# A second pair of PSUM banks for some landmark products, products with v grouped by tile shape, and another order of steps

## The chip, the cores and the metric

The kernel runs on one core of one Trainium2 chip. Its time is the device time of one execution in microseconds (us), as the median of three runs. Beside these runs there is one profiled execution, whose trace gives every instruction of the five engines (TensorE or PE with its weight loads PEld, VectorE or DVE, ScalarE or ACT, GpSimd or POOL, SyncE or SP) and the clock that was granted to TensorE.

## The reference

Three stages are computed in a row, all in float32: a Nystrom attention of 8 batches with 8 heads, 576 tokens and 64 features, then a gated layer, then a layer with an ELU.

```python
# q, k, v: (8, 8, 576, 64); 32 landmarks = means over 18 tokens
q_lm = q.reshape(B, H, 32, 18, D).mean(axis=3)
k_lm = k.reshape(B, H, 32, 18, D).mean(axis=3)
A, Bm, C = sm(q, k_lm), sm(q_lm, k_lm), sm(q_lm, k)     # softmax of scaled products
Z = Bm.T / (norm1(Bm) * norminf(Bm) + 1e-6)             # largest sums of columns and of rows, per head
for _ in range(6):
    Z = 2 * Z - Z @ Bm @ Z
x = A @ Z @ C @ v                                       # to (4608, 512)
h = ((x @ w1) * (x @ w2)) @ w3                          # 512 -> 1024 -> 1024
x = h @ w_out                                           # 1024 -> 512
h = x @ w_in                                            # 512 -> 2048
out = np.where(h > 0, h, np.exp(np.minimum(h, 0)) - 1) @ w_out2   # 2048 -> 512
```

## The kernel before

The kernel has a start, a first layer and a second layer. In the start the weights come from DRAM and are converted (steps `L`, `y`, `r`, `h`, `w`, `x` of one weight tile each: load, two passes on ScalarE, two on VectorE, one on GpSimd), and the product of w3 and w_out is formed once in 16 groups (`o`, L908). Batch 0's attention is worked in between.

The first layer runs over 128 units u, 16 of each batch. A unit is two groups of 12 full-array products of 288 columns: `A` (function `ab`, the two gated products, in the two PSUM banks of the pool `ps_mm`) and `Y` (`yy`, accumulated over 8 units in four banks of `ps_acc`). Between them the gated product is taken off PSUM: `G` (ScalarE copies the first bank), `g` (VectorE multiplies with the second), `D` and `d` (high and low part). The next `A` may write the first bank after `G` and the second after `g`.

Among the units stands the attention of the following batch, written `:b` and a letter. On TensorE these are small products on tiles of part of the array: `c0`, `c1` (landmarks of q with all of k, tile 64x32), `a0`, `a1`, `t0` to `t2` (transposes, full array), `v0`, `v1` (the products with v: 128 and, for the last 64 tokens, 64 rows high, 32 wide), `z`, `m0` to `m3` (the landmark products with the gated layer's weights, tile 64x32, 512 columns, two banks each), and for pairs of batches `b`, `r`, `n0` to `n5` (32 wide). Before the change all of them write the two banks of one pool, `ps_at`: `c1` can write when `C0` (ScalarE) has read `c0`, and `m1` when `M0` (ScalarE, high part) and `l0` (VectorE, low part) have read `m0`. A visit below is one or more small products in a row between full-array groups.

In the second layer the activations are read back from DRAM (`yin`, L1141) and split in parts `YH`/`YL`; rows `R` (L1196 to L1198) are six full-array products each for one of 40 units, rows `OR` (L1290 to L1292) the six products of the output side. Their weights come as `wp` tiles (`WP`, four buffers, queued on SyncE, L1135) and `wh` tiles (queued on GpSimd). `OP` and `OE` add a row's bank to the sums on VectorE, and `OO` stores a result from SyncE's queue.

Every engine works its instructions in the order in which they are written. That order is one list, STEPS: 4418 steps, whose functions are called one after the other. Which of two or three buffers a tile takes is written in a second list, SLOTS; a name that isn't in it takes the buffers in turn. A step that waits holds up all that stands behind it on its engine.

Of the kernel before, what the change touches and what calls it, by code (L numbers as in the profile page):

```python
# [52 lines left out]
h17 o11 r17 r20 o13 :0r :0ce1 h20 r16 L18 :0bx y21 :0R o15 s0 h21 w20 s1 :0ae x16 L19 s2 r21 w17 S0 S1 :0n0 S2
:0N0 w21 s3 x17 S3 :0iv :0au y19 L23 o16 h19 y18 x21 w19 r19 x19 L25 :0af0 :0a1 x20 o17 :0A1 y22 :1iq h22 r22
r25 L27 h18 r23 :0n1 :3S0 y25 o19 w18 h25 w25 r18 :0N1 :0n2 L24 :0am y23 y27 :0as :1k0 :0ae h23 w23 L30 h27
:0N2 L29 y30 :1k2 x25 r27 :0ah0 w27 x18 w22 L26 h30 L33 o21 x23 :0t2 :1q0 y24 :1q3 x27 :0n3 :0T2 x22 y29 r30
L31 h29 r24 o23 :0N3 w30 :0t1 h24 :0T1 y26 w24 x24 :1k3 r26 :0n4 :0N4 y31 h26 w26 :0cn x30 L34 :3L1 y34 h31
o25 r29 L28 x26 :1q2 w31 y33 :0v0 :1k1 L32 :0v1 w29 :0V y28 x29 :0n5 h28 r31 :0N5 w28 x31 r28 o27 h33 w33 :0z
r33 x33 :0Z :0au h34 :3L2 :3S2 o29 w34 :1q1 :0m0 y32 x28 r34 = L35 s4 L39 s7 S7 x34 s6 :0M0 :0l0 r35 :0H0 :0m1
h32 :1p0 :3S1 y35 h35 r32 :0M1 w32 A0 G0 :0l1 y39 g0 x32 h39 :1b A1 G1 s5 r39 :1B w35 w39 D0 L38 x39 g1 S4  # L60
:1c0 :1C0 S5 A2 x35 G2 S6 g2 :1c1 d0 y38 D1 :1C1 D2 d1 r38 h38 A3 :1cm0 :1be G3 L36 :0m2 w38 Y0 Y1 r36 d2 y36
h36 :0M2 L37 g3 x38 D3 :0l2 :2ik A4 :1iv w36 :0af1 G4 g4 :1a0 y37 h37 w37 :1A0 :1am :1cm1 x36 D4 r37 x37 A5 G5
# [48 lines left out]
A102 :7T0 d99 d100 P0 :7t2 G102 g102 P1 P1 d101 A103 G103 :7t1 :7cn :7T2 Y99 :7T1 g103 P0 P0 Y100 A104 P0 G104
# [1446 lines left out]
```

## Time and profile before

| | before |
|---|---|
| median of 3 runs | 1324.06 us (1323.56 to 1324.64) |
| the profiled execution | 1323.18 us |
| its span in the trace | 1321.4 us |
| TensorE busy in the span | 1289.0 us (98%) |
| VectorE, ScalarE, GpSimd busy | 1044.5, 792.6, 565.4 us |
| mean granted TensorE clock | 0.995 of 2.4 GHz |

About 1.8 us of the execution lie outside the span. In a timeline row the first number is the start in us from the span's start, the second the time to the end of the group; since products are pipelined, what a group costs is read from start to start. A bracket at a row's end is the idle time of that engine before the row and what ended it.

### The profile page before, as it was taken

The page shows a single profiled execution, that of the slowest core. Times are in us where ns is not written, and L with a number is a line of the kernel's source. Part 1 is how long each engine was busy: PE and PEld are TensorE (multiplying, and loading weights), DVE is VectorE, ACT ScalarE, POOL GpSimd, SP SyncE. Part 2 cuts the span into 40 slices and gives each one's busy share as a digit, 9 for nine tenths or more (in the row PEclk, how much of TensorE's full clock was granted, in tenths as well). Part 3 has the DMA queues.
Part 4 walks back from the last instruction along what each step waited for, and adds up shares of the span by engine and source line. Part 5 has one row for each costly group of instructions (what it writes and reads, how often), then busy time and mean ns, then how long its engine had stood idle before and what let it go on. Part 6 is the DMA issues. An engine that isn't in the chain of part 4 may idle for free.

```text
span 1321.4 us, 24443 instructions
## 1 busy us (share of the span) xinstructions
PE 1289.0 (98%) x9456; PEld 1096.1 (83%) x9456; DVE 1044.5 (79%) x1680; ACT 792.6 (60%) x1433; POOL 565.4 (43%) x511
## 2 busy tenths in 40 slices
PE   5989999999999999999999999999999999999998
PEld 2448888989898889899999887887888888888997
DVE  6998867687768766554899867897778987898878
ACT  6566444554455445445768585766758667666764
POOL 4552436564655537131552434334323344333333
PEclk9999999999999999999999999999999999999999
DMA  8954536773675354254867575466565765467855
GB/s 318 318 178 161 185 131 221 266 227 118 226 261 187 125 185 150 106 196 158 321 231 270 226 259 195 167 239 233 204 222 180 250 248 206 137 228 249 300 195 174
DMA packets 81587, 279.19 MB, mean 211 GB/s; under 512 B 7232, under 2 KB 32832, under 8 KB 73280
## 3 DMA queue, kind: packets, MB, share of 16 engines
q1 hardware_dynamic: 75712, 204.24, 44.6%
q0 software_dynamic: 5760, 73.40, 15.2%
q8 instruction: 74, 1.21, 0.4%
q14 instruction: 41, 0.34, 0.1%
HBM read 229.38 MB, written 48.23 MB: 210 GB/s over the span
## 4 chain that ended last, share of the span: by engine, by line
PE 83%; DVE 7%; DMA 2%; issue 1%; ACT 1%; POOL 0%; SPq 0%; DVEq 0%; POOLq 0%; ACTq 0%
PE h L1196 8%; PE h L1198 8%; PE h L1197 8%; PE o L1291 8%; PE o L1290 8%; PE o L1292 8%; PE ab L1051 6%; PE y L1086 5%; PE ab L1052 5%; PE ab L1053 5%; PE y L1087 5%; PE y L1088 5%; PE m L645 2%; DVE el L1269 2%; DMA wp<-wo_d 1%
## 5 line engine op out<-in xcount | busy, mean ns | idle before, releaser
L1290 PE MATMUL o<-eh,wp 128*128 128x512 f32 (+1 forms) x560 | 207.6, 371 | 6.3 <-DVE oa L1308 3.6
L1291 PE MATMUL o<-el,wp 128*128 128x512 f32 (+1 forms) x560 | 207.5, 370 | 1.0 <-DVE el L1269 1.0
L1292 PE MATMUL o<-eh,wp 128*128 128x512 f32 (+1 forms) x560 | 207.2, 370 | 0.0
L1197 PE MATMUL h<-yb,wh 128*128 128x512 f32 (+1 forms) x560 | 206.4, 369 | 0.8 <-DVE yb L1176 0.8
L1196 PE MATMUL h<-yb,wh 128*128 128x512 f32 (+1 forms) x560 | 206.7, 369 | 0.1
L1198 PE MATMUL h<-yb,wh 128*128 128x512 f32 (+1 forms) x560 | 206.8, 369 | 0.0
L1253 POOL TENSOR_TENSOR tt<-g,tt 128x512 f32<-128x512 f32 (+1 forms) x80 | 107.2, 1344 | 167.6 <-DVE el L1269 164.9
L1051 PE MATMUL ab<-ath,mh 128*128 128x288 f32 x512 | 157.5, 308 | 0.0
L1086 PE MATMUL y<-gh,w3oh 128*128 128x288 f32 x512 | 155.3, 303 | 0.0
L1052 PE MATMUL ab<-atl,mh 128*128 128x288 f32 x512 | 151.2, 295 | 0.0
L1053 PE MATMUL ab<-ath,ml 128*128 128x288 f32 x512 | 151.0, 295 | 0.0
L1087 PE MATMUL y<-gl,w3oh 128*128 128x288 f32 x512 | 150.8, 295 | 0.1
L1088 PE MATMUL y<-gh,w3ol 128*128 128x288 f32 x512 | 150.6, 294 | 0.0
L1253 POOL TENSOR_TENSOR tt<-g,g 128x512 f32<-128x512 f32 (+1 forms) x40 | 51.4, 1284 | 209.1 <-DVE g L1245 162.4
L1216 ACT COPY g<-h 128x512 f32<-128x512 f32 (+1 forms) x160 | 86.3, 541 | 82.8 <-PE h L1198 80.4
L1269 DVE TENSOR_TENSOR el<-g,eh 128x512 fp32r<-128x512 f32 (+1 forms) x160 | 120.3, 769 | 10.4 <-ACT eh L1264 10.1
L1290 PEld LDWEIGHTS o<-eh,wp 128*128 128x128 f32 x560 | 105.5, 188 | 23.7 <-DVE oa L1308 6.4
L1059 ACT COPY a<-ab 128x288 f32<-128x288 f32 x128 | 51.0, 398 | 119.5 <-PE ab L1053 95.3
L1218 DVE TENSOR_TENSOR g<-h,g 128x512 f32<-128x512 f32 (+1 forms) x120 | 75.9, 633 | 59.0 <-PE h L1198 55.3
L1241 DVE SCALAR_TENSOR_TENSOR t<-m,t 128x1024 f32<-128x1024 f32 (+1 forms) x80 | 102.5, 1281 | 21.5 <-ACT m L1237 21.1
L1291 PEld LDWEIGHTS o<-el,wp 128*128 128x128 f32 x560 | 105.5, 188 | 16.5 <-DVE el L1269 2.4
L1051 PEld LDWEIGHTS ab<-ath,mh 128*128 128x128 f32 x512 | 96.3, 188 | 26.3 <-issue 13.1
(154 smaller groups left out, 3119.7 us busy)
## 6 DMA issues: line engine op xcount, KB each, us to landing
wh<-wh_d POOLq DMA_DIRECT2D x40, 1792.0 KB, 8.0
wp<-wo_d SPq DMA_DIRECT2D x140, 512.0 KB, 4.5
wo_raw<-in_w_out_dram SPq DMA_DIRECT2D x24, 512.0 KB, 5.2
q<-in_qT_dram SPq DMA_DIRECT2D x8, 1152.0 KB, 6.3
k<-in_kT_dram SPq DMA_DIRECT2D x8, 1152.0 KB, 7.3
yd<-ysb SPq DMA_DIRECT2D x15, 576.0 KB, 3.8
w_raw<-in_w3T_dram SPq DMA_DIRECT2D x16, 512.0 KB, 6.5
w_raw<-in_w_dram SPq DMA_DIRECT2D x16, 512.0 KB, 4.9
```

Of the source, the lines that this page charges most:

```text
L1051: pe.matmul(p[:, :NH], mh[:, cs], ah[:, blk, :], start=(blk == 0), stop=False)
L1052: pe.matmul(p[:, :NH], mh[:, cs], al[:, blk, :], start=False, stop=False)
L1053: pe.matmul(p[:, :NH], ml[:, cs], ah[:, blk, :], start=False, stop=(blk == 1))
L1086: pe.matmul(a[oc][:, :NH], w3o_hi[fc][:, os_], gh, start=(fc == 0), stop=False)
L1087: pe.matmul(a[oc][:, :NH], w3o_hi[fc][:, os_], gl, start=False, stop=False)
L1088: pe.matmul(a[oc][:, :NH], w3o_lo[fc][:, os_], gh, start=False, stop=(fc == K1 - 1))
L1196: pe.matmul(o, ah, bh[:, kk, :], start=first and kk == 0, stop=False, skip_group_check=True)
L1197: pe.matmul(o, ah, bl[:, kk, :], start=False, stop=False, skip_group_check=True)
L1198: pe.matmul(o, al, bh[:, kk, :], start=False, stop=(kk == 1), skip_group_check=True)
L1290: pe.matmul(o, w[:, d, 0, cs], eh, start=first and d == 0, stop=False, skip_group_check=True)
L1291: pe.matmul(o, w[:, d, 0, cs], el, start=False, stop=False, skip_group_check=True)
L1292: pe.matmul(o, w[:, d, 1, cs], eh, start=False, stop=(d == 1), skip_group_check=True)
```

## The change

The function `ps` of the attention takes a flag; with it the tile comes from `ps_mm` (the banks of `A`) and not from `ps_at`. `c1`, `m1` and `m3` set the flag. The steps `v0` and `v1` divide the products with v in another way: before, `v0` was one head of each pair and `v1` the other, each through all five chunks of tokens; now `v0` is both heads through the four chunks of 128 tokens, and `v1` both through the last of 64. STEPS holds the same 4418 steps in another order, and SLOTS has no entries for the tiles that went to `ps_mm`, so these take the two banks in turn with `A`. Nothing else differs.

```diff
-        def ps(self, nm):
-            return ps_at.tile([128, 512], F32, name=f"{nm}_{self.b}", tag="at")
+        def ps(self, nm, second=False):
+            pool_, tag = (ps_mm, "mm") if second else (ps_at, "at")
+            return pool_.tile([128, 512], F32, name=f"{nm}_{self.b}", tag=tag)
...
-        def pair_scores(self, nm, small, big, cols):
-            ps = [self.ps(f"{nm}{i}") for i in range(2)]
+        def pair_scores(self, nm, small, big, cols, second=False):
+            ps = [self.ps(f"{nm}{i}", second) for i in range(2)]
...
-            self.cps[n] = self.pair_scores(f"c{n}", ..., slice(n * NH, (n + 1) * NH))
+            self.cps[n] = self.pair_scores(f"c{n}", ..., slice(n * NH, (n + 1) * NH), n == 1)
...
-        def cv(self, blk):
+        def cv(self, part):
...
-            for c in range(5):
+            for c in range(4) if part == 0 else (4,):
                 kc = 128 if c < 4 else 64
-                for j in range(4):
+                for blk in range(2):
+                    for j in range(4):
...
-                        start=(c == 0), stop=(c == 4),
+                            start=(c == 0 and blk == 0), stop=(c == 4 and blk == 1), skip_group_check=True,
...
-            self.mps[jn] = self.pair_scores(f"m{jn}", self.z, w12_sb, slice(jn * 512, (jn + 1) * 512))
+            self.mps[jn] = self.pair_scores(f"m{jn}", self.z, w12_sb, slice(jn * 512, (jn + 1) * 512), jn % 2 == 1)
...
-:6ae :6au Y89 A93 G93 :6a1 g93 A94 Y90 D91 d91 G94 D92 :6af0 :6A1 :6ah0 :6H0 :6m1 g94 :6am A95 d92 Y91 G95 g95
+:6l0 P0 G92 g92 D92 A93 :6a1 P0 G93 g93 A94 P1 :6ae :6au :7iq P0 P0 Y90 Y91 :6af0 G94 g94 :6m1 :6M1 :6A1 :6m2
```

In the program's listing of TensorE around `m1` and `m2` of batch 6, `m10_6` and `m11_6` are the two banks of `m1`, `m20_6` and `m21_6` those of `m2`, `ab95` is `A95`, `y510` to `y513` the sums of a `Y`. Before:

```order
L1088 MATMUL y513_6754<-gh90_6714,w3ol2_92 128x288
L645 MATMUL m10_6_6883<-w12_sb_98,z_6_6649 32x512
...
L645 MATMUL m11_6_6884<-w12_sb_98,z_6_6649 32x512
L1051 MATMUL ab95_0_6896<-ath51_6424,mh5_3_0_6003 128x288
...
L1053 MATMUL ab96_1_6934<-ath60_6879,ml6_0_1_6748 128x288
L645 MATMUL m20_6_6960<-w12_sb_98,z_6_6649 32x512
...
L645 MATMUL m21_6_6961<-w12_sb_98,z_6_6649 32x512
L1086 MATMUL y510_6751<-gh92_6871,w3oh4_86 128x288
```

After:

```order
L1085 MATMUL y513_6749<-gh91_6762,w3ol3_93 128x288
L641 MATMUL m10_6_6897<-w12_sb_98,z_6_6612 32x512
...
L641 MATMUL m11_6_6898<-w12_sb_98,z_6_6612 32x512
L641 MATMUL m20_6_6916<-w12_sb_98,z_6_6612 32x512
...
L641 MATMUL m21_6_6917<-w12_sb_98,z_6_6612 32x512
L1083 MATMUL y510_6746<-gh92_6807,w3oh4_86 128x288
...
L1085 MATMUL y513_6749<-gh92_6807,w3ol4_94 128x288
L1048 MATMUL ab95_0_6950<-ath51_6384,mh5_3_0_6003 128x288
```

Before, each of the two stood alone between full-array groups; now they are neighbours, and one `Y` stands between them and the next `A`, which writes the banks of `m1`.

ScalarE where the second layer's first activations come: `a116` is the copy `G116`, `yb002` and `yb005` are the first parts taken from the tile `yin0` that is being read from DRAM. Before:

```order
L742 CAST mh7_3_0_8073<-m30_7_7976 128x512
L742 CAST mh7_3_1_8076<-m31_7_7977 128x512
L1059 COPY a117_8097<-ab117_0_8044 128x288
L1069 CAST gh116_8101<-a116_8022 128x288
L1172 CAST yb002_8132<-yin0_8000 128x2x384
L1059 COPY a118_8136<-ab118_0_8106 128x288
```

After:

```order
L1056 COPY a115_8025<-ab115_0_7985 128x288
L1066 CAST gh115_8028<-a115_8025 128x288
L1169 CAST yb005_8053<-yin0_8051 128x2x384
L1056 COPY a116_8056<-ab116_0_8037 128x288
L1066 CAST gh116_8071<-a116_8056 128x288
L1056 COPY a117_8093<-ab117_0_8079 128x288
```

The first part now stands ahead of the copy `G116`, before ahead of `G118`.

SyncE's queue at the end of the second layer's first block: `out_0_dram<-oa..` are stores that wait for VectorE, `wp8_0` is the first weight tile of the next block. Before:

```order
L1135 DMA wp6_6_9946<-wo_d_71 128x1024
L1320 DMA out_0_dram<-oa01_8665 128x384
L1320 DMA out_0_dram<-oa11_8667 128x384
L1135 DMA wp8_0_10017<-wo_d_71 128x1024
L1135 DMA wp8_1_10045<-wo_d_71 128x1024
L1320 DMA out_0_dram<-oa10_8666 128x384
```

After:

```order
L1132 DMA wp6_6_9898<-wo_d_71 128x1024
L1317 DMA out_0_dram<-oa01_8619 128x384
L1132 DMA wp8_0_9990<-wo_d_71 128x1024
L1132 DMA wp8_1_9993<-wo_d_71 128x1024
L1317 DMA out_0_dram<-oa00_8618 128x384
L1317 DMA out_0_dram<-oa11_8621 128x384
```

Two stores stood ahead of `wp8_0`; now one does.

## Rows read from the trace of the kernel before

**Rows 1.** Two stretches: length, busy PE, PEld, DVE, ACT, POOL; clock, DMA.

```profile
120.00:560.00 440.00, 439.75 (x5007) 384.84 (x5007) 321.78 (x650) 211.21 (x497) 227.75 (x238) 1.00 0.54 181
756.00:760.00 4.00, 3.87 (x11) 3.31 (x12) 2.81 (x5) 0.69 (x2) 2.99 (x3) 0.57 0.53 163
```

**Rows 2.** Timeline of TensorE at the end of the start.

```profile
86.23 1.09 PE L645 MATMUL m<-w_sb,z 64*32 64x512 f32 x16
90.69 2.55 PE L645 MATMUL m<-w_sb,z 64*32 64x512 f32 x16 [3.37 <-DVE ml L747]
93.17 0.61 PE L1051 MATMUL ab<-ath,mh 128*128 128x288 f32 x1
```

**Rows 3.** Timeline of TensorE around one `m` between full-array products.

```profile
210.91 0.29 PE L1052 MATMUL ab<-atl,mh 128*128 128x288 f32 x1
211.04 0.29 PE L1053 MATMUL ab<-ath,ml 128*128 128x288 f32 x1
211.26 1.09 PE L645 MATMUL m<-w_sb,z 64*32 64x512 f32 x16
212.28 0.40 PE L1051 MATMUL ab<-ath,mh 128*128 128x288 f32 x1
212.52 0.30 PE L1052 MATMUL ab<-atl,mh 128*128 128x288 f32 x1
```

**Rows 4.** What TensorE waited for in the second layer: in total, times, longest (us).

```profile
PE o L1290 <- DVE oa L1308: 3.6, 3, 1.8
PE o L1290 <- DMA wp<-wo_d: 2.6, 2, 2.0
```

**Rows 5.** Timeline of TensorE: one `n` alone, then `n` and `v` together.

```profile
191.24 0.65 PE L885 MATMUL n<-X 32*32 32x64 f32 x32
191.82 0.40 PE L1086 MATMUL y<-gh,w3oh 128*128 128x288 f32 x1
...
193.60 0.65 PE L885 MATMUL n<-X 32*32 32x64 f32 x32
194.18 1.73 PE L706 MATMUL cv<-v,ct 128*32 128x64 f32 x80
195.84 0.40 PE L1086 MATMUL y<-gh,w3oh 128*128 128x288 f32 x1
```

**Rows 6.** Timeline of TensorE in the start: an `n` of half as many products.

```profile
59.14 0.43 PE L885 MATMUL n<-X 32*32 32x64 f32 x16
59.50 3.70 PE L908 MATMUL w3acc<-wo,w 128*128 128x512 f32 x8
63.13 0.43 PE L885 MATMUL n<-X 32*32 32x64 f32 x16
```

**Rows 7.** Stretches within one `v0` `v1`, L706 alone: length, PE, PEld; clock, DMA.

```profile
257.87:258.29 0.42, 0.42 (x30) 0.42 (x32) 1.00 1.02 188
258.29:258.70 0.41, 0.41 (x27) 0.23 (x15) 1.00 0.93 380
```

**Rows 8.** Timeline of TensorE, ScalarE and VectorE after a later `m`.

```profile
547.74 0.40 PE L1086 MATMUL y<-gh,w3oh 128*128 128x288 f32 x1
547.90 1.07 ACT L742 CAST mh<-m 128x512 fp32r<-128x512 f32 x2 [0.28 <-PE m L645]
549.71 1.28 DVE L747 TENSOR_TENSOR ml<-m,mh 128x512 fp32r<-128x512 f32 x2
```

**Rows 9.** Timeline of SyncE and ScalarE where `yin` is first read.

```profile
563.71 0.58 SPq L1141 DMA_DIRECT2D yin<-yd  x1
571.30 0.84 ACT L1172 CAST yb<-yin 128x768 fp32r<-128x768 f32 x1 [1.32 <-DMA yin<-yd]
```

**Rows 10.** Timeline of SyncE and TensorE at the second layer's first block end.

```profile
741.78 6.13 SPq L1320 DMA_DIRECT2D out_dram<-oa  x2
748.01 1.26 SPq L1135 DMA_DIRECT2D wp<-wo_d  x2
756.13 0.64 PE L1290 MATMUL o<-eh,wp 128*128 128x512 f32 x1 [1.99 <-DMA wp<-wo_d]
```

More of the change, by code (lines that the diff above doesn't have):

```diff
@@ L53 @@
[L53 to L62, printed above, removed]
@@ L113 @@
-A107 G107 :7A0 :7m0 P1 Y102 D105 Y103 d105 g107 P0 :7am D106 :7M0 :7as P0 P0 Y104 P0 :7ae D107 A108 G108 P0
-:7l0 P0 d106 g108 :7a1 P0 P1 A109 d107 :7au Y105 Y106 D108 d108 G109 g109 D109 :7af0 P0 P0 P0 A110 G110 g110
-Y107 A111 d109 :7A1 :7am :7ah0 :7m1 G111 Y108 :7as :7ae :7M1 :7au g111 D110 d110 D111 :7H0 A112 Y109 :7l1 :7m2
-:7af1 G112 g112 D112 A113 P0 P0 Y110 G113 P0 P1 g113 A114 d111 G114 g114 d112 Y111 C111.0 A115 :7M2 :7l2 :7m3
-P0 D113 G115 :7ah1 :7H1 C111.1 2 ly g115 A116 D114 d113 C111.2 G116 g116 C111.3 d114 Y112 A117 Y113 D115 CO111
@@ new lines @@
+D106 g108 A109 :7ae d106 G109 Y105 g109 A110 :7au D107 :7m0 d107 G110 g110 D108 d108 A111 :7M0 :7l0 Y106 G111
+g111 :7a1 :7af0 :7A1 Y107 D109 :7ah0 :7H0 :7am d109 :7m1 :7M1 :7as :7l1 :7m2 :7ae :7au Y108 D110 P0 P0 A112
+:7M2 G112 g112 A113 d110 Y109 D111 G113 g113 A114 d111 Y110 :7af1 G114 P0 :7ah1 :7H1 D112 D113 :7l2 g114 d112
+:7m3 :7M3 Y111 C111.0 C111.1 :7l3 A115 C111.3 d113 C111.2 Y112 D114 d114 P0 P0 P1 P0 G115 g115 D115 d115 2
+A116 ly YH0.5 G116 g116 Y113 D116 d116 SY0.0 A117 G117 Y114 g117 D117 A118 G118 Y115 CO111 g118 YL0.5 YH0.0
@@ new lines @@
+GH6.0.6 M9.0 P10.2 R10.4 GH8.0.0 GH8.1.0 P10.3 OP6.5.0 GL6.0.6 OR6.6.0 OE0.1.0 WP8.0 GL8.1.0 WP8.1 GL8.0.0
+OR8.0.1 SY2.0 LW11 OE0.2.0 S8.0 S8.2 OE0.1.1 OE0.2.1 OO0.0.0 OO0.1.1 GH8.0.1 t9.1 e9.1 OR8.0.0 SY2.2 x9.1
+GH8.1.1 OR6.6.1 R10.5 M9.1 OP8.0.1 P10.4 GH8.0.2 P10.5 S8.1 OO0.1.0 OP8.0.0 m10.0 R10.6 OE0.3.0 S9.0 GL8.0.1
+GH8.0.3 GH8.1.2 S9.2 R11.0 S9.1 P10.6 t10.0 e10.0 R11.1 GL8.1.2 GL8.1.1 OR8.1.1 GL8.0.3 OE0.3.1 GH8.1.3
+GL8.1.3 P11.0 WP8.2 OR8.1.0 OP8.1.1 WP8.3 OR8.3.1 GL8.0.2 OP8.1.0 GH8.1.4 GL8.1.4 OR8.2.0 OP8.3.1 OR8.2.1
@@ new lines @@
+GL14.0.0 OP12.4.0 OR12.5.0 GH14.0.1 YL2.5 M15.0 P16.1 OP12.5.1 OR12.6.1 OP12.5.0 S14.2 GH14.1.0 GL14.1.0
+WP14.0 WP14.1 GL14.0.1 GH14.0.2 GL14.0.2 OR14.0.1 OR14.0.0 YL2.1 R16.2 YL2.4 LW17 t15.1 e15.1 GH14.0.3 x15.1
+GH14.1.1 GL14.1.1 R16.3 P16.2 M15.1 R16.4 P16.3 S15.0 S15.1 R16.5 OP14.0.1 WP14.2 OR14.1.1 OP14.0.0 P16.4
+OP14.1.1 GH14.1.2 WP14.3 WP14.4 OR14.1.0 WP14.5 GL14.1.2 LY3 OR14.2.1 OP14.1.0 OR14.2.0 YH2.6 GH14.1.3
+GL14.1.3 GH14.0.4 m16.0 t16.0 YL2.6 GL14.0.3 GH14.0.5 GL14.0.4 GL14.0.5 S15.2 GH14.1.4 GL14.1.4 P16.5 R16.6
@@ new lines @@
+GH18.0.2 GL18.0.2 R21.0 P20.6 R21.1 LW22 OP18.0.0 WP18.1 WP18.2 WP18.3 OR18.1.0 GH18.1.2 m20.0 OP18.0.1
+OR18.1.1 GH18.0.3 GL18.1.2 OR18.2.0 t20.0 e20.0 GH18.1.3 WP18.4 WP18.5 OP18.1.0 GL18.1.3 GL18.0.3 P21.0
+OR18.2.1 OP18.1.1 x20.0 M20.0 GH18.0.4 GH18.0.5 GL18.0.4 GL18.0.5 OR18.3.1 OR18.3.0 R21.2 GH18.1.4 P21.1
+OP18.3.1 m20.1 t20.1 e20.1 GH18.1.5 R21.3 x20.1 M20.1 S18.3 P21.2 R21.4 GL18.1.5 P21.3 S19.3 GH18.1.6 P21.4
+m21.0 t21.0 S20.0 S20.1 R21.5 OP18.3.0 R21.6 P21.6 GL18.1.4 OR18.4.0 e21.0 OR18.4.1 GL18.1.6 P21.5 S20.2
@@ new lines @@
+GL20.1.3 YH3.2 S21.2 YH3.0 YL3.2 OR20.2.0 OR20.2.1 OR20.3.1 WP20.5 GH20.0.4 GH20.0.5 OP20.1.0 OR20.3.0
+GH20.1.4 P23.0 YL3.0 GL20.0.5 GH20.1.5 S20.3 P23.1 R23.2 GL20.1.5 GH20.0.6 GL20.0.4 OP20.3.0 P23.2 WP20.6
+R23.3 P23.3 OP20.3.1 R23.4 YH3.4 S21.3 GL20.1.4 R23.5 M22.1 GH20.1.6 P23.4 R23.6 GL20.0.6 OR20.4.1 P23.5 YH3.5
+YL3.5 m23.0 OP20.4.1 WP22.0 t23.0 OR20.4.0 e23.0 S22.0 S22.2 GL20.1.6 OP20.4.0 LW24 YH3.6 YH3.3 OR20.5.1
+OP20.5.1 OR20.6.0 OR20.5.0 x23.0 GH22.0.0 M23.0 P23.6 m23.1 OR20.6.1 YL3.3 R24.0 GL22.0.0 YH3.1 YL3.1 R24.1
@@ new lines @@
+OE2.3.0 R26.6 m26.0 P26.5 S24.2 OO2.0.0 R27.0 S24.1 M25.1 S25.0 S25.1 GL24.1.1 LW28 P26.6 GH24.1.2 R27.1
+WP24.2 P27.0 WP24.3 OO2.3.0 GL24.1.0 OR24.0.1 OO2.0.1 P27.1 GL24.1.2 GL24.0.2 OR24.0.0 OP24.0.1 OR24.1.1 t26.0
+OO2.1.0 OP24.0.0 OR24.1.0 e26.0 x26.0 GH24.1.3 GL24.1.3 GH24.0.3 OE2.3.1 OR24.2.0 OR24.2.1 M26.0 OP24.1.1
+m26.1 GL24.0.3 R27.2 OP24.1.0 OR24.3.0 GH24.0.4 GL24.0.4 OO2.3.1 GH24.0.5 GL24.0.5 OP24.3.0 t26.1 S25.2
+GH24.1.4 GL24.1.4 OR24.3.1 S24.3 e26.1 WP24.4 x26.1 OP24.3.1 M26.1 GH24.0.6 P27.2 R27.3 R27.4 WP24.5 P27.3
@@ L288 @@
+OE4.0.0 GL38.1.3 GL38.0.4 S39.2 GH38.1.4 GL38.1.4 WP38.4 OR38.2.1 OR38.3.0 GH38.0.5 OP38.3.0 GL38.0.5 OR38.3.1
+GH38.1.5 GL38.1.5 OO4.0.0 OP38.3.1 WP38.5 WP38.6 OR38.4.0 OR38.4.1 OE4.0.1 OP38.4.0 OR38.5.0 S38.3 GH38.0.6
+GL38.0.6 OP38.4.1 OO4.0.1 S39.3 OR38.5.1 GH38.1.6 GL38.1.6 OP38.5.0 OR38.6.0 OE4.1.0 OO4.1.0 OP38.5.1 OE4.2.0
+OO4.2.0 OE4.3.0 OO4.3.0 OR38.6.1 OE4.1.1 OE4.2.1 OO4.1.1 OO4.2.1 OE4.3.1 OO4.3.1
 """
@@ L340 @@
+c01_5:0 ct1_5:1 ct0_5:0 ct2_5:0 cv_5:0 z_5:1 a00_5:0 a01_5:1 m00_5:0 m01_5:1 a10_5:0 a11_5:1 m20_5:0 m21_5:1
+bs_6:0 c00_6:1 c01_6:0 r0_6:1 ct0_6:0 n0_6:1 ct1_6:0 n1_6:1 n2_6:0 ct2_6:1 n3_6:0 n4_6:1 cv_6:0 n5_6:1 z_6:1
+a00_6:0 a01_6:1 m00_6:0 m01_6:1 a10_6:0 a11_6:1 m20_6:0 m21_6:1 c00_7:0 c01_7:1 ct0_7:0 ct1_7:1 ct2_7:0 cv_7:0
+z_7:1 a00_7:0 a01_7:1 m00_7:0 m01_7:1 a10_7:0 a11_7:1 m20_7:0 m21_7:1 h0:0 h1:1 slice_3:01010101
+slice_5:01010101 slice_7:10101101
 """
```

467 lines of the change are left out of this document (220 added, 247 removed).

## The prediction

> **What bounds the kernel now.** I read the stretches by stage first, then what TensorE waited for, then its timeline at single visits. Through the first layer TensorE is busy 439.75 of 440.00 us, VectorE 321.78 and ScalarE 211.21 [rows 1]. So nothing is late there: the layer's time is the sum of what TensorE has in its queue, and a change gains there only by making that queue shorter. The waits stand elsewhere: one of 3.37 us at the end of the start, after which the next products run slowly (2.48 us from start to start for an `m` that takes 1.02 later) [rows 2, 3], and in the second layer two kinds, 3.6 us in three waits for VectorE to empty a bank and 2.6 us in two for a weight tile [rows 4].
>
> What can be shorter in a queue that is always full is seen at one visit. Full-array products start 0.13 us apart; the `m` starts 0.22 after the last of them and the second product after it 0.24 behind the first [rows 3]. A visit thus pays 0.09 at its entry and 0.11 at its exit, together 0.195 us, beside its own 1.02.
>
> **The change part by part.** The sum is made against the profiled execution, 1323.18 us (span 1321.4 and 1.8 around it); the median shown is 0.9 above it, which I add at the end.
>
> *Merged visits.* I counted neighbours in the listing of TensorE's order from the first `A` on. Before, 10 times a small product follows another small one (transposes, which use the full array, left out); after, 33 times. Each of the 23 new pairs saves one entry and one exit, if a pair of different shapes costs nothing between them. The trace has such a pair: `n` (32x32) takes 0.58 us to the start of what follows, both alone before a full-array product and ahead of `v` (128x32), and `v` then takes 1.66 [rows 5]. Nothing extra stands between. 23 x 0.195 = 4.5 us.
>
> The Trainium skill's page "TensorEngine Tiling (Array Packing)", section "Tiling Modes", Key Properties, says that changing the tiling mode drains the engine and changing only the tile doesn't. By that rule a pair of two shapes would still pay one of its two changes, so 9 of the 23 pairs would be worth 0.1 less, 0.9 us in all; the pair in rows 5 shows no such payment, so the sum does without it.
>
> *Pairs of one shape.* 14 of the 23 are of one shape (seven `m` `m`, five `c` `c`, two `m` `c`). Within a visit doubling the products is cheaper than a second visit: an `n` of 16 records takes 0.36 us [rows 6], one of 32 0.58 and not 0.72 [rows 5]. The 0.14 saved is the part that a shape pays once. 14 x 0.14 = 2.0 us; the ends are nothing, if the change of banks brings it back, and 2.4.
>
> *Products with v.* Of one `v0` the first 32 records (128 rows high) take 0.42 us, the other 8 (64 rows high) 0.41, though they are a quarter as many [rows 7]; in these 0.41 lie the change to the smaller tile and the change back. After, a batch has 64 records of the first kind (0.84) and then 16 of the second: 0.41 and 8 more at 0.42/32 each, 0.10. That is 1.35 against 1.66, 0.31 saved in each of seven batches, 2.1 us. If the 0.41 is not the change but the small products themselves, nothing is saved; if a second set adds nothing, 2.9.
>
> *End of the start.* Before, `m1` waits for `l0` and `A0` starts at 93.17. After, `m1` follows `m0` at once, and `A0` must wait for `l1`. With `m0` at 86.23 as before: it ends at 87.25, four copies of 0.53 behind it end at 89.5 and the last subtraction of 0.64 at 90.2 at the earliest [rows 2, 8]. If VectorE is as late as before, where `l0` ended at 90.69, `l1` adds 1.28 and ends at 92.0. Between these I take 91.3, a gain of 1.9 us. The list of the start is new too, so `m0` itself can move; I bound that by one group of `o` of 3.63 us [rows 6] to either side, since PE's work ahead of `m0` is the same, and leave the middle at zero.
>
> *Banks of `A` lent out.* This is the wait that the change adds. From the first `A` on, `c1` seven times, `m1` seven times and `m3` eight times hold the banks that the next `A` needs, and all that TensorE has behind that `A` waits with it. Seven of the fifteen `m` have only one `Y` as cover: 12 x 0.13 = 1.6 us to the first bank, 2.4 to the second, which `A` writes half a unit later. What is needed: after an `m` that ended at 547.74, ScalarE's copies ended at 548.97 and VectorE's subtractions at 550.99, since a product and a low part of other units stood before them [rows 8]. With VectorE free they would end at 549.7, 1.9 us after the `m`: no wait. As in that row, 3.2 us: a wait of 0.8 to 1.0. The ends over 22 places are 0 and some 16; nearer to the prompt case, because VectorE has a quarter of its time free [rows 1], I take 3 us.
>
> *First read of `yin`.* The load was issued at 563.71, the first part taken from it at 571.30, after ScalarE had idled 1.32 us for it [rows 9]. After, that part stands two copies of `A` earlier in ScalarE's queue, ahead of `G116`; behind it wait `G116`, the product `g116` and with them `A117`. If the load is issued where it was against the units (after the last `m3`, five groups before `A117`), it lands 7.6 us later against 8.0 us of groups (5 x 12 x 0.133). The part of 0.84 us comes on top and behind it the copy, 288 columns to its 768, so 0.3: 0.7 us late, 0.8 with the step from engine to engine. Ends 0 and 3, take 0.8.
>
> *Weight tiles in the second layer.* `wp8_0` was queued behind two stores that held SyncE for 6.13 us; it was issued at 748.01 and TensorE stood still until 756.13 [rows 10]. After, one store is ahead of it, and by the listing eight us of rows at least stand between its release and its use, for the tile of before 3.8. The wait of 1.99 us goes, and with it the slow stretch: the granted clock was 0.57 from 756 to 760 [rows 1], of the two levels half the time 1.2 and not 2.4 GHz, which cost 4 x 0.43 = 1.7. Together 3.6 us; at worst nothing.
>
> *The rest of the second layer* is reordered without any shorter work. Its waits for VectorE (3.6 us [rows 4]) may fall away or double; a new order brings some of its own. I add 1.0, with ends of -3 and +4.
>
> Sum: 4.5 + 2.0 + 2.1 + 1.9 + 3.6 = 14.1 gained, 3.0 + 0.8 + 1.0 = 4.8 given back, 9.3 in all. 1323.2 - 9.3 = 1313.9, and with 0.9 for the median 1314.8 us.
>
> **The rivals.** *Merging is worth half.* Shapes and banks pay their way between neighbours: the 2.0 and the 2.1 are nothing and the mixed pairs give 0.9 less. For it speaks that no row shows two neighbours of one shape in different banks; against it rows 5. 1314.8 + 5.0 = 1319.8.
>
> *The new order gives it back elsewhere.* The wait for a weight tile returns at another block with its slow stretch (3.6), the start gains nothing (1.9), `yin` comes 3 us late (2.2 more). For it: SyncE's stores stand in the same queue as before, and the list was made without seeing this chip's delays. Against: the shortest distance between a tile's release and its use is 5.2 us of rows in both listings once the one at `wp8_0` is left out. 1314.8 + 7.7 = 1322.5.
>
> *The lent banks decide.* If VectorE is one conversion step further behind at the seven `m` with one `Y` as cover than in rows 8, 1.3 us on top of the 1.0 there, each costs 2.3: 16.1 instead of 3.0, and 1327.9 us. It decides from a mean of 1.4 us at the 15 `m`, where the 9.3 and the 3.0 are used up and more. For it: conversion steps do stand in VectorE's queue among these units. Against: 118 us of 440 are free there.
>
> *It doesn't do what it says.* In the listing two of the eight `c0` `c1` are not neighbours; the counts above are already of those that are.
>
> **How the numbers follow.** The forecast has 0.62, the first rival 0.18, the second 0.12, the third 0.08. The forecast's own range is 1309.5 (the start 2.6 earlier, no wait at the lent banks) to 1319; with the first and part of the second rival the range is 1309.5 to 1322. Within 0.2% of the time before, which is about what a measurement of this kernel can tell from no change, lies 1321.4 to 1326.7: most of the second rival and an edge of the first, 0.11. Slower is the third rival, 0.08, faster 0.81.
>
> **What would show it.** Right: `m1` and `m2` in the trace as neighbours that together take about 1.9 us; `v` at 1.35 a batch; `A0` near 91; the stretch of the first layer without idle time on TensorE above 3 us; no wait for `wp` near 750. Wrong: waits of `ab` for `ml` or `a` of more than 0.3 us each, a wait of `A117` above 2, or a slow clock after a new wait in the second layer. If the small pairs cost as much as two visits the first two terms are gone, and if TensorE idles at every lent bank the sign turns.

## The result and the profile after

The changed kernel takes 1313.6 us (median of four runs, 1312.54 to 1314.8), beside 1324.3 us of the kernel before, measured with it; the ratio is 0.9919 with an interval of 0.9907 to 0.9932. The forecast was 1314.8. Run once more on another chip, the ratio was 0.9952 (0.9934 to 0.9970), 1316.8 us beside 1323.46. The two intervals don't meet, so a ratio from one chip doesn't settle a term of 1 to 4 us; the forecast gain of 9.3 lies between the two that were measured, 10.7 and 6.7. Why it is not the same number each time is part of what follows. The profiled execution took 1313.6 us, its span is 1311.8.

To see where the 9.7 us between the two profiled executions come from, I charged each product in TensorE's timeline with the time to the start of the next one, less the idle time in its bracket, and summed by part (us):

| | before | after | difference |
|---|---|---|---|
| start of `A0` | 93.17 | 90.24 | -2.93 |
| products of the first layer from there on | 514.62 | 509.55 | -5.07 |
| TensorE's waits among them | 0.22 | 2.63 | +2.41 |
| products of the second layer | 700.67 | 698.34 | -2.33 |
| TensorE's waits among them | 8.00 | 6.23 | -1.77 |
| start of the last product | 1316.68 | 1306.99 | -9.69 |

The pairs first. In the timeline of TensorE after the change (start, time to the end of the group, engine, line, product, tile, shape, count, and in brackets the idle time before it) two `m` are one group of 32, and so are two `c`; they answer to the `m` alone in [rows 3].

```profile
153.11 0.29 PE L1085 MATMUL y<-gh,w3ol 128*128 128x288 f32 x1
153.33 1.95 PE L641 MATMUL m<-w_sb,z 64*32 64x512 f32 x32
155.21 0.40 PE L1083 MATMUL y<-gh,w3oh 128*128 128x288 f32 x1
155.45 0.30 PE L1084 MATMUL y<-gl,w3oh 128*128 128x288 f32 x1
...
236.55 0.29 PE L1085 MATMUL y<-gh,w3ol 128*128 128x288 f32 x1
236.77 1.20 PE L641 MATMUL c<-k,qsum 64*32 64x288 f32 x32
237.90 0.41 PE L1083 MATMUL y<-gh,w3oh 128*128 128x288 f32 x1
238.14 0.30 PE L1084 MATMUL y<-gl,w3oh 128*128 128x288 f32 x1
```

What a visit costs is the time between the starts of the second full-array product behind it and of the last one ahead of it, less the 0.27 that two of these take anyway. The pair of `m` costs 155.45 - 153.11 - 0.27 = 2.07; one `m` in [rows 3] costs 212.52 - 211.04 - 0.27 = 1.21, two of them 2.42. So 0.35 are saved. The pair of `c` costs 1.32, a single `c` before cost 0.84: 0.36 saved. Products with v, which took 1.66 to the next start in [rows 5], now take 1.39, and two `n` around them cost no second entry:

```profile
194.94 0.65 PE L882 MATMUL n<-X 32*32 32x64 f32 x32
195.52 1.46 PE L703 MATMUL cv<-v,ct 128*32 128x64 f32 x80
196.91 0.45 PE L882 MATMUL n<-X 32*32 32x32 f32 x32
```

A pair of two shapes, an `m` and a `bs` (tile 128x32), costs 423.11 - 421.24 - 0.27 = 1.60, beside 1.21 and 0.58 for the two alone: 0.19 saved, about half as much. Behind it the `m` of another visit, which has a `c` of its own tile behind it:

```profile
421.24 0.29 PE L1085 MATMUL y<-gh,w3ol 128*128 128x288 f32 x1
421.47 1.09 PE L641 MATMUL m<-w_sb,z 64*32 64x512 f32 x16
422.49 0.46 PE L809 MATMUL bs<-ksum,qpad 128*32 128x32 f32 x32
...
423.11 0.29 PE L1084 MATMUL y<-gl,w3oh 128*128 128x288 f32 x1
...
162.28 1.09 PE L641 MATMUL m<-w_sb,z 64*32 64x512 f32 x16
163.16 0.74 PE L641 MATMUL c<-k,qsum 64*32 64x288 f32 x16
```

Summed over all visits from `A0` on, less the waits inside them, the small products cost 106.5 us before and 98.2 after, 8.3 us less (0.45 of it is one `bs` that now stands ahead of `A0`).

The end of the start, which answers to [rows 2]: `m0` begins where it did (86.45 for 86.23), `m1` follows at once, and `A0` waits for the second low part.

```profile
86.45 2.04 PE L641 MATMUL m<-w_sb,z 64*32 64x512 f32 x32 [1.23 <-DVE z L730]
89.05 0.33 PE L809 MATMUL bs<-ksum,qpad 128*32 128x32 f32 x16 [0.56 <-DVE ml L744]
90.24 0.40 PE L1048 MATMUL ab<-ath,mh 128*128 128x288 f32 x1 [0.86 <-DVE ml L744]
```

The two stretches that stand against [rows 1] (length; busy PE, PEld, DVE, ACT, POOL with counts; granted clock, DMA share, GB/s): the queue is as full as before, but a stretch near its beginning runs at 0.76 of 2.4 GHz with 1.5 us idle.

```profile
120.00:560.00 440.00, 439.65 (x5044) 391.33 (x5043) 325.24 (x656) 216.24 (x506) 228.36 (x239) 1.00 0.54 184
105.00:112.00 7.00, 5.50 (x28) 5.21 (x28) 6.67 (x21) 3.16 (x9) 2.81 (x2) 0.76 0.72 275
```

What happened there stands in ScalarE's timeline and TensorE's:

```profile
104.05 0.67 ACT L952 ACTIVATE w_y<-w_raw 128x512 bf16<-128x512 bf16 x1 [2.69 <-DMA w_raw<-in_w_dram]
105.19 0.38 ACT L1056 COPY a<-ab 128x288 f32<-128x288 f32 x1
...
105.62 0.40 PE L1048 MATMUL ab<-ath,mh 128*128 128x288 f32 x1 [0.68 <-ACT a L1056]
107.57 0.40 PE L1048 MATMUL ab<-ath,mh 128*128 128x288 f32 x1 [0.89 <-DVE a L1061]
```

ScalarE stood 2.69 us at the conversion `y37` (the first row) for a weight load still in flight. The copy `G4` behind it came late, and `A5` and `A6` with it. Seventeen full-array products then started some 0.24 us apart, which cost 1.84 us beyond their usual 0.13.

The longest of what TensorE waited for from `A0` on, and the one wait for `oa` that is left (in total, times, longest). The first three lines and the last belong to the second layer, those for `wp` and `oa` answer to [rows 4]; `ml` is the wait of `A0` shown above and the only one at a lent bank:

```profile
PE o L1287 <- DMA wp<-wo_d: 2.4, 2, 1.5
PE o L1287 <- DVE el L1266: 1.7, 1, 1.7
PE h L1193 <- DVE g L1215: 1.5, 2, 1.0
PE ab L1048 <- ACT a L1056: 1.4, 2, 0.7
PE ab L1048 <- DVE ml L744: 0.9, 1, 0.9
PE o L1287 <- DVE oa L1305: 0.2, 1, 0.2
```

### The profile page after: what moved, and what is told of

Same layout as the page of the kernel before. It is cut to its first block, busy times and chain, and to the rows that moved or that the text cites. A ratio compares the mean times of both kernels' runs of the same rounds, so it can differ in the third digit from the quotient of the medians.

```text
span 1311.8 us, 24405 instructions
## 1 busy us (share of the span) xinstructions
PE 1278.8 (97%) x9456; PEld 1098.3 (84%) x9456; DVE 1037.7 (79%) x1680; ACT 795.6 (61%) x1433; POOL 567.1 (43%) x511
## 3 DMA queue, kind: packets, MB, share of 16 engines
q8 instruction: 74, 1.21, 0.4%
## 4 chain that ended last, share of the span: by engine, by line
PE 84%; DVE 5%; DMA 3%; ACT 1%; issue 1%; POOL 0%; ACTq 0%; DVEq 0%; POOLq 0%; SPq 0%
PE h L1193 8%; PE h L1195 8%; PE h L1194 8%; PE o L1287 8%; PE o L1289 8%; PE o L1288 8%; PE ab L1048 6%; PE y L1083 6%; PE y L1084 5%; PE y L1085 5%; PE ab L1050 5%; PE ab L1049 5%; PE m L641 2%; DVE el L1266 2%; DMA wh<-wh_d 1%; PE n L882 1%
## 5 line engine op out<-in xcount | busy, mean ns | idle before, releaser
L1266 DVE TENSOR_TENSOR el<-g,eh 128x512 fp32r<-128x512 f32 (+1 forms) x160 | 126.6, 810 | 14.1 <-ACT eh L1261 13.9
L1193 PEld LDWEIGHTS h<-yb,wh 128*128 128x128 f32 x560 | 105.1, 188 | 18.0 <-DVE g L1215 2.7
L1061 DVE TENSOR_TENSOR a<-ab,a 128x288 f32<-128x288 f32 x128 | 57.6, 450 | 76.5 <-PE ab L1050 44.1
```

The lines of the kernel that those rows point to most:

```text
L1193: pe.matmul(o, ah, bh[:, kk, :], start=first and kk == 0, stop=False, skip_group_check=True)
```

## The experiments

Each kernel here was compared with the kernel before on the same chip, in five rounds: e1, e3, e4 and e5 on one chip, e6 to e9 on a second, e10 and e11 on a third. Runs of one kernel scatter by up to 13.5 us (e4_split), so a term of 1 or 2 us is read from the profiled execution, by the parts of the table above:

| | ratio to before | `A0` | first layer | waits | second layer | waits |
|---|---|---|---|---|---|---|
| changed, again (e10_after) | 0.9952 (0.9934 to 0.9970) | 91.09 | 509.80 | 3.34 | 699.40 | 6.21 |
| e1_old_v | 0.9948 (0.9929 to 0.9967) | 91.63 | 509.59 | 2.76 | 699.75 | 5.72 |
| e3_no_cover | 1.0016 (0.9999 to 1.0033) | 92.28 | 513.19 | 10.88 | 699.31 | 6.23 |
| e4_split | 0.9978 (0.9959 to 0.9997) | 90.58 | 510.80 | 5.05 | 702.03 | 7.95 |
| e5_first_only | 0.9975 (0.9966 to 0.9984) | 89.96 | 507.85 | 2.93 | 699.73 | 10.15 |
| e6_w37 | 0.9926 (0.9909 to 0.9944) | 90.95 | 507.77 | 1.82 | 699.79 | 6.40 |
| e7_loads | 0.9953 (0.9935 to 0.9972) | 91.65 | 509.07 | 3.02 | 700.56 | 6.24 |
| e8_all | 0.9930 (0.9903 to 0.9957) | 90.30 | 508.22 | 1.42 | 699.21 | 3.79 |
| e9_v_only | 0.9984 (0.9975 to 0.9993) | 93.23 | 514.28 | 0.55 | 700.42 | 7.76 |
| e11_next | 0.9886 (0.9862 to 0.9910) | 90.53 | 508.04 | 0.33 | 701.23 | 9.25 |

**The products with v, once taken back and once alone.** The body of `cv` is exchanged, in e1_old_v as shown and in e9_v_only the other way round; e1_old_v also moves batch 0's `v0`, in the start, next to its `v1`:

```diff
-        def cv(self, part):
-            for c in range(4) if part == 0 else (4,):
-                for blk in range(2):
+        def cv(self, blk):
+            for c in range(5):
```

> The changed kernel with the products with v divided as before (one head of each pair through all five chunks, then the other); order, banks and all else as changed. My theory: each batch pays the change to the 64-row tiles twice again, 1.86 us a visit and not 1.58, eight batches, so +2.2 us: 1315.8 against 1313.6 of the changed kernel. Rival, the 0.41 us of the eight 64-row products is their own length and not the change of tile: nothing, 1313.6, and 1.58 stays for the visit.

> The kernel before with the new division of the products with v alone; its order of steps, its banks and all else as before. My theory: 1.58 us for 1.86 in each batch, eight batches, 2.0 to 2.2 us less where v0 and v1 stand together, less where another product parts them; 1322 against 1324.1 of the kernel before. Rival, the 64-row products cost what they cost and nothing is saved: 1324. And whether the full-array products of the first layer still start every 0.1325 us, as in the profile of before, or every 0.1329, as in the profile of the changed kernel, tells whether that difference (1.2 us over 3072 of them) belongs to the order of steps or to the run.

In the changed kernel the old division costs 1.94 us more in the sum of the visits that hold a `cv` (15.05 to 16.99); in the kernel before the new one costs 1.90 less (15.09 to 13.19), 0.27 in each of seven batches, and its ratio of 0.9984 is 2.1 us. A visit of `cv` alone shows it, first the changed kernel, then the old division in the changed kernel's order:

```profile
385.21 0.29 PE L1050 MATMUL ab<-ath,ml 128*128 128x288 f32 x1
385.43 1.46 PE L703 MATMUL cv<-v,ct 128*32 128x64 f32 x80
386.82 0.40 PE L1048 MATMUL ab<-ath,mh 128*128 128x288 f32 x1
```

```profile
514.35 0.29 PE L1037 MATMUL ab<-ath,ml 128*128 128x288 f32 x1
514.57 1.73 PE L690 MATMUL cv<-v,ct 128*32 128x64 f32 x80
516.23 0.40 PE L1070 MATMUL y<-gh,w3oh 128*128 128x288 f32 x1
```

1.39 against 1.66 us to the next start. The rival that nothing is saved is out. The time of e1_old_v itself decides nothing: its scatter (1311.55 to 1322.27) is larger than the term. And with the old order the full-array products of the first layer start every 0.1325 us again, in all ten profiles with the new order every 0.1328 or 0.1329; so this difference, 1.2 us over 3072 products, belongs to the order. What in it makes it I don't know.

**The pairs apart, and the pairs without cover.** In six batches, of which batch 1 is shown, e4_split sets the second `m` behind the next group (first line with +), e3_no_cover both directly ahead of the next `A` (second):

```diff
-:1m1 :1m2 d13 Y13 D14 D15 P0 P0 d14 :1M1 :1l1 A16
+:1m1 d13 Y13 :1m2 D14 D15 P0 P0 d14 :1M1 :1l1 A16
+d13 Y13 D14 D15 P0 P0 d14 :1m1 :1m2 :1M1 :1l1 A16
```

> The changed kernel with m1 and m2 of six batches apart again: the second of the two stands behind the next full-array group. Banks and all else as changed. My theory: six visits more, each one entry, one exit (0.195) and the shared part of one shape (0.155, from 2 x 1.21 - 2.07): +0.35 each, +2.1 us: 1315.7. Rival, shapes and banks pay their way between neighbours, so that apart costs only 0.1 more each: 1314.2.

> The changed kernel with the pair m1, m2 of six batches put directly ahead of the next A, behind the Y groups that stood between. My theory: a lent bank costs nothing only as long as a Y covers its copies; here the A behind waits for the high and low part of m1, with m2 alone (1.0 us) as cover, 0.9 to 2.2 us at each of six places, 5 to 13 us in all, more if TensorE's clock falls after these waits: 1319 to 1327. Rival, VectorE has time enough and the pair is as cheap anywhere: 1313.6 with waits of ab for ml under 0.3 us.

Apart, the visits cost 2.1 us more (100.3 for 98.2), 0.35 a pair: my 0.35 and not the rival's 0.1. Beside that one `A` waited 1.45 us for a lent bank, since the moved `m` took its cover. The time itself, 1320.4 for the 1315.7 expected, doesn't measure the edit: in the profile the second layer, which the edit leaves alone, took 5.4 us more than in the changed kernel (702.03 + 7.95 against 698.34 + 6.23).

Without cover the kernel is no faster than before (1.0016). Here is what TensorE waited for in that kernel, and the worst place in the timelines of TensorE, VectorE and ScalarE:

```profile
PE ab L1036 <- DVE ml L732: 6.8, 7, 2.1
PE y L1072 <- DVE gl L1060: 1.9, 3, 0.9
```

```profile
416.49 1.07 ACT L727 CAST mh<-m 128x512 fp32r<-128x512 f32 x2 [0.58 <-PE m L629]
417.26 1.40 DVE L612 TENSOR_REDUCE qsum<-q 128x32 f32<-128x576 f32 x2
418.58 1.28 DVE L732 TENSOR_TENSOR ml<-m,mh 128x512 fp32r<-128x512 f32 x2
419.31 0.40 PE L1036 MATMUL ab<-ath,mh 128*128 128x288 f32 x1 [2.06 <-DVE ml L732]
```

Of the seven waits one is that of `A0`; the six others take 0.6 in four places, under the 0.9 expected as the least, 1.46 in batch 3, where `m1` stands behind `m2` and has no cover at all, and 2.06 where other work of VectorE stood before the subtraction, 5.9 in all. With the waits of `Y` for `gl` and more slow products the first layer takes 11.9 us more than in the changed kernel (513.19 + 10.88 against 509.55 + 2.63). Both sums lie within the 5 to 13 expected. So the lent bank is not free; one `Y` is what pays for it.

**The first layer of the new order, the second of the old.** The list is cut at the step `p2`, which opens the second layer.

```diff
-p2 WP0.0 GH0.0.0 x0.1 M0.1 S0.0 R1.1 P1.1
+p2 GH0.0.0 R1.1 x0.1 M0.1 S0.0 S0.2 R1.2
```

> The changed kernel up to the end of the first layer, and from there on the steps in the order before the change (the two lists hold the same steps on both sides of that point). My theory: the gain of the second layer, 4.1 us by the rows of the two profiles (2.3 in slow products, 1.8 in waits), goes, with the wait for the weight tile near 750 and the slow stretch behind it back: 1317.7. Rival, the second layer's gain came from how the first layer hands over and not from its own order: 1313.6 to 1315.

The second layer then takes 709.9 us with its waits for 704.6, so 5.3 us of the gain are its own order's; by the ratios, from other chips, it is 3 us beside e10_after and 7 beside the first measurement. All three waits for `oa` of [rows 4] are back, and so is the one for the weight tile, but this time nothing ran slowly behind it, the granted clock was 1.00:

```profile
PE o L1275 <- DMA wp<-wo_d: 3.9, 3, 2.4
PE o L1275 <- DVE oa L1293: 3.6, 3, 1.8
```

```profile
750.00:754.00 4.00, 3.90 (x18) 3.42 (x19) 3.54 (x7) 2.20 (x4) 3.39 (x3) 1.00 0.57 183
```

**The new wait at 105 us.** Three steps of one weight tile (`y37`, `h37`, `w37`) go behind `G4`, where its other two stood already:

```diff
-P1 P0 y37 h37 :1cm0 x39 r36 w37 w36 A4 G4 :3L2 :1a0 g4 :1A0 r37 x37 :1am
+P1 P0 :1cm0 x39 r36 w36 A4 G4 :3L2 :1a0 g4 :1A0 y37 h37 r37 w37 x37 :1am
```

> The changed kernel with the conversion of one weight tile (y37, h37, r37, w37, x37) put behind the copy G4 and the transposes A0 of batch 1 in the list, nothing else moved. My theory: in the changed kernel ScalarE stood 2.7 us at y37 for a weight load that was still in flight, with G4 behind it, so A5 and A6 waited 0.68 and 0.89 us (1.3 and 0.9 in later profiles) and the clock could fall behind them, 0.4 to 1.8 us: the waits go, 2.0 to 3.6 us less, 1310.0 to 1311.6 against 1313.6. Rival, the waits come from the lent banks of m1 and c1 there: they stay, 1313.6. Second rival, the tile is late for m3 and the wait moves there: 1313.

The waits of `A5` and `A6` are gone and the clock from 104 to 112 is 1.00; `m3` waits 0.83 for the tile instead, so the second rival has a part. The first layer with its waits takes 2.6 us less than in the changed kernel (509.6 for 512.2), the ratio is 3.4 us below that of e10_after, though the intervals meet, and no lower than that of the first measurement (0.9919). So the gain is shown in the profile and not in the time. The wait came from the load, not from the lent banks.

**The second layer's loads.** `WP0.6` goes ahead of `LY1`, `WP6.2` ahead of `LY2`, `YH0.5` behind `G117`; e8_all has this and the move above.

```diff
-OR4.6.1 OR4.6.0 e7.1 LY2 GH6.0.1 LW9 GH6.0.2 YH1.6 OP4.5.1 WP6.2 WP6.3
+OR4.6.1 OR4.6.0 e7.1 WP6.2 LY2 GH6.0.1 LW9 GH6.0.2 YH1.6 OP4.5.1 WP6.3
```

> The changed kernel with three steps moved: the weight tiles WP0.6 and WP6.2 ahead of the loads LY1 and LY2 of the second layer's activations in SyncE's queue, and the first part YH0.5 behind G117. My theory: both loads held SyncE 6.6 and 9.0 us for a buffer, and the two weight tiles behind them reached TensorE 0.90 and 1.48 us late; YH0.5 kept A117 0.74 us. These go, and perhaps the 1.66 us behind the second: 3.1 to 4.8 us less, 1308.8 to 1310.5. Rival, the tiles are late because they share the DMA engines with the activations wherever they stand in the queue: only 0.7 less, 1312.9.

> The moves of the two kernels before this one in the list together. My theory: they lie in different stretches where TensorE is the bound, so their gains add: 5 to 8 us less than the changed kernel, 1305.5 to 1308.5. Rival, what is gained in the first layer is lost at the second layer's loads, which then come earlier against the same data rates: no better than the better of the two.

The wait of `A117` went and both tiles came in time, so the rival is out for these two; but my gain isn't there either: 6.24 us of waits in the second layer for 6.23, and a median of 1316.46. The wait at 646 is gone, but the one for VectorE behind it grew from 1.02 to 2.31 us (at 655), and another weight tile came 1.23 late at 671, which e8_all with the same second layer doesn't show. The wait for VectorE is the same in e8_all; its timeline of GpSimd and VectorE (the first two are sums `S2.2` and `S2.1`, the last is `SY1.1`) shows why:

```profile
645.20 1.03 POOL L1237 TENSOR_TENSOR g<-g,g 128x384 f32<-128x384 f32 x1
645.57 4.41 DVE L1253 TENSOR_TENSOR el<-g,eh 128x384 fp32r<-128x384 f32 x1
646.18 1.02 POOL L1237 TENSOR_TENSOR tt<-g,tt 128x384 f32<-128x384 f32 x1
647.15 2.40 POOL L1146 TENSOR_TENSOR tv<-yin,tv 128x1024 f32<-128x1024 f32 x1
...
650.76 0.55 DVE L1202 TENSOR_TENSOR g<-h,g 128x384 f32<-128x384 f32 x1
651.37 0.44 PE L1180 MATMUL h<-yb,wh 128*128 128x384 f32 x1 [2.15 <-DVE g L1202]
```

An `el` that takes 0.55 us took 4.41, and ended 0.43 after GpSimd's third instruction. e8_all as a whole has not shown my sum: its median of 1313.42 is no better than e6_w37's 1313.07, as the rival had it. Three of its runs took 1308.9 to 1309.5 and three 1317 to 1319, so the rival isn't shown either.

**The GpSimd sum moved.** From e8_all, `x36` goes ahead of `x37`, and `SY1.1` from here to behind `S3.1`.

```diff
-r37 w37 x37 :1am :3L3 A5 D3 D4 :1ce0 G5 x36 Y2
+r37 w37 x36 x37 :1am :3L3 A5 D3 D4 :1ce0 G5 Y2
-R4.5 SY1.1 M3.1 GH2.1.1 GL2.1.1 R4.6 S3.0
+R4.5 M3.1 GH2.1.1 GL2.1.1 R4.6 S3.0
```

> The kernel with the moves of the conversion and of the three loads, and two more: x36 ahead of x37 in GpSimd's queue, so that m3 need not wait 1.1 us for it, and the sum SY1.1 (2.4 us on GpSimd) behind S3.1. My theory: a VectorE instruction with both inputs in SBUF stands still as long as GpSimd works instruction after instruction; el at 645.6 us took 4.41 us and not 0.55 while GpSimd ran two sums and SY1.1, and TensorE waited 2.15 us for what came behind. With SY1.1 later, el ends when the two sums do, after some 2.4 us, and TensorE's wait at 651 falls to 0.2 or less: with the 1.1 and the slow stretch behind (1.6) 3 to 5 us less than the kernel with the moves alone, whose undisturbed runs took 1309; 1304 to 1306, or some 7 below the changed kernel beside it. Rival, el is long for another reason (its input is late, or TensorE's rows are the bound): 651 still waits 2 us, and 1308.

> The changed kernel once more, nothing altered, on the same chip and beside the same runs of before as the next kernel: its ratio to before should fall in 0.991 to 0.994, and the waits of A5 and A6 at 106 to 110 us stand in every profile while the slow stretch behind them comes in some only.

```profile
644.28 1.03 POOL L1237 TENSOR_TENSOR g<-g,g 128x384 f32<-128x384 f32 x1
644.44 2.27 DVE L1253 TENSOR_TENSOR el<-g,eh 128x384 fp32r<-128x384 f32 x1
645.26 1.02 POOL L1237 TENSOR_TENSOR tt<-g,tt 128x384 f32<-128x384 f32 x1
```

`el` ends with the two sums, after 2.27 us (2.4 expected), TensorE waits for nothing near 650, and in the first layer 0.33 us of waits are left. This is the fastest version: 0.9886 to the changed kernel's 0.9952 on the same chip, 8.7 us (some 7 expected), and the intervals don't meet. Its times are 1304.68 to 1307.35 in three runs and 1312.98 to 1315.95 in the others, so its median of 1310.17 misses the 1304 to 1306 expected. The profiled one is the slowest: ScalarE waited 5.1 us for a store to have read `oa` before it could overwrite it, and TensorE 3.35 for that, near 913. In e4_split, e6_w37 and e8_all ScalarE has such a wait too, of 1.5 to 2.0 us, and TensorE none for it. Why the store was late in this execution stays open. The changed kernel run again missed its expected 0.991 to 0.994; the waits of `A5` and `A6` stood there (1.38 and 0.90 us), with a slow stretch behind them and a second one at 727.

## Why the prediction was right, step by step

- **Merged visits, pairs of one shape, products with v** (4.5 + 2.0 + 2.1 = 8.6): measured 8.3 over all visits, 7.9 without the `bs`; of it 1.9 is the products with v. The pair of one shape was worth 0.35 a place, as entry, exit and the shared part had given (0.195 + 0.14), and e4_split and e9_v_only hold these sizes. A pair of two shapes saved 0.19, as forecast, but not because nothing stands between. From start to start an `m` takes 1.02 us ahead of `bs` (422.49 - 421.47), as it does ahead of a full-array product in [rows 3], and only 0.88 ahead of a `c` of its own tile (163.16 - 162.28). So the change to another small tile cost 0.14, like the change to the full array. In [rows 5] the 0.58 of `n` is the same in both places because a change stands behind it in both, and my reading that nothing is paid there was wrong. What I called the shared part of one shape is that payment: a pair of one tile saves two changes (0.35), a pair of two tiles one (0.19), and the new division of the products with v, which has two changes fewer, 0.27. The Trainium skill, "TensorEngine Tiling (Array Packing)", section "Tiling Modes", has a change of mode drain the engine. The trace agrees, with 0.14 to 0.19 us a change. The sum came out all the same, since 0.195 for every new pair and 0.14 more for those of one shape add up to about the same.
- **End of the start** (1.9): 2.9. `A0` began at 90.24 where I had 91.3, at the early end of what I had bounded (90.2). In the ten profiles that share this start it lies between 89.96 and 92.28, so the step holds, and its spread of 2.3 us is a part of the scatter.
- **Banks lent out** (3.0 given back): mis-sized, 0. No `A` behind the first waited for `ml` or for `e`. I had taken the price of a place from rows where VectorE was busy; in the new order the subtractions came in time. At all seven `m` with one `Y` as cover the first low part ended 0.2 us before the `A` began; at one of them the `m` ended at 489.65, its low parts at 491.12 and 491.72, and the `A` began at 491.34. That is the prompt case of the forecast, at every place. e3_no_cover shows the term itself: 0.6 to 2.1 us a place when the cover is gone.
- **First read of `yin`** (0.8): 0.74, at the place I named.
- **Weight tiles in the second layer** (3.6): the wait at 750 and the slow stretch went, but waits of 0.90 and 1.48 for `wp` came at two other blocks, and 1.66 for `el`. **The rest of the second layer** (1.0 lost) gained instead, since the three waits for `oa` shrank from 3.6 to 0.2. Together 2.6 forecast, 4.1 measured (2.33 + 1.77).
- **Not in the forecast:** the wait at the conversion `y37`, 1.57 us and 1.84 of slow products behind it, 3.4 in all, nearly what I had set aside for the lent banks. I had looked at what `A` waits for through the banks and not at what stands ahead of its copy in ScalarE's queue. By my own signs (a wait of `ab` for `a` above 0.3 us) these waits of 0.68 and 0.89 counted as a sign of being wrong. Also the 1.2 us of the slightly longer distance between products. By these parts some tenths of a microsecond of the first layer stay unplaced.

Two readings of the prediction need to be set right, and neither moves its sum. The clock of 0.57 from 756 to 760 is not half the time at 1.2 GHz but some 86% of it; the 1.7 us worked out from it hold. And the third rival decides at a mean of 0.8 us over 15 places (9.3 + 3.0), not at 1.4.

So the time came out within 1.2 us partly by luck, with two terms that were wrong in opposite directions: 3.0 us set aside that were not needed, and 3.4 that were needed elsewhere. The second measurement lies 2.0 us on the other side. Of the larger terms only the gain of the small products was foreseen to a few tenths. Its rival, half of that, fell with e4_split and e9_v_only.

## What to carry to other kernels

Where TensorE's queue is always full, price a small product by its visit, from the last large product ahead to the second behind: count the changes of tile in it, to and from the full array and between small tiles alike, at 0.14 to 0.19 us each here, and put products of one tile next to each other first. A bank lent to make neighbours is paid by the work that stands between the loan and the next owner, so look for that cover first and then for what stands ahead of the copies in the other queues, loads included. After such a gain, look at GpSimd: a VectorE instruction that takes many times its usual length can explain a wait of TensorE for a later one.

## What the runs showed of the hardware

VectorE can stand still for GpSimd far longer than one instruction. In the row of e8_all `el` reads two tiles in SBUF and held on through three GpSimd instructions in a row (4.41 us for 0.55); in e11_next through two (2.27). The wait of 1.66 us for `el` at 728.6 in the changed kernel is, by its rows, of this kind too; no run tested it. VectorE worked without a pause from the long `el` here to the one that TensorE waited for:

```profile
720.51 3.40 DVE L1266 TENSOR_TENSOR el<-g,eh 128x384 fp32r<-128x384 f32 x1
720.54 1.98 POOL L1250 TENSOR_TENSOR tt<-g,tt 128x384 f32<-128x384 f32 x2
722.49 1.00 POOL L1250 TENSOR_TENSOR g<-g,g 128x384 f32<-128x384 f32 x1
```

The kernel before had its share: of the three waits for `oa` in [rows 4] the one at 826 stands behind a VectorE instruction of 4.78 us, usually 1.22, beside three GpSimd sums from 819.6 to 823.4. The Trainium skill, "SBUF — State Buffer", section "Who interferes with whom", says that the port pair shared by VectorE and GpSimd is an exclusive lock, that a VectorE instruction with two SBUF inputs contends with a GpSimd instruction that reads SBUF, and that issue order decides who blocks. The rows agree that it blocks and doesn't share; that the loser can lose again to the next instruction is what they add. In the last rows `el` is even recorded 0.03 us ahead of the first GpSimd instruction, and lost; spans on GpSimd are rough.

A wait of TensorE does not always cost its clock. The waits near 106 us stand in seven profiles; in four of them 13 to 17 products behind ran at about half speed (1.45 to 1.84 us), in three only three products did (0.4 us). The same wait for a weight tile at 750 was followed by 1.8 us of slow products in the kernel before and by none in e5_first_only. In these profiles such a stretch came or didn't behind the same wait, and why stays open; with the start it is a part of why runs of one kernel differ.
